# Loading the output weight ahead of the second chunk's v, in a fused attention and feed-forward kernel

## Chip, cores, metric

One core of one Trainium2 chip. The metric is the device time of one execution in microseconds (us). PE is TensorE (PEld its weight loads), DVE VectorE, ACT ScalarE, POOL GpSimd, SP SyncE. The executions whose state is on record are of the fast state, with a granted TensorE clock of 0.999 to 1.0.

## The reference

```python
def _attn_ref(q, k, v, tau):                       # q, k, v: (4, 6144, 256)
    qn = q / (np.linalg.norm(q, axis=1, keepdims=True) + 1e-06)
    kn = k / (np.linalg.norm(k, axis=1, keepdims=True) + 1e-06)
    s = kn.transpose(0, 2, 1) @ qn / tau           # 256 x 256 per batch
    ...                                            # softmax over the last axis
    return (v @ a).astype(np.float32)

def _moe_ref(x, w1, w2, w3, w_out):                # x: (24576, 256), d_ff 768
    h = np.maximum(np.maximum(x @ w1, x @ w2), x @ w3)
    return (h @ w_out).astype(np.float32)
```

## The kernel before

Per batch, a small gram product gives the attention matrix, which is folded into the three weights (`aw`). Then 48 chunks of 512 tokens stream by: load v (cast to bf16), transpose it, multiply by the three folded weights, take the maximum (`h_block`), multiply by the output weight `wo_sb` (`o_steps`). The output products of chunk n run between the hidden blocks of chunk n+1. All casting loads go out on GpSimd's queue; the transposes are DMA transposes issued by SyncE. The first chunk is transposed on PE.

The guard matters here: a one-element copy on GpSimd that reads the end of a transposed tile. The loads written after it go out only once it has run: in the trace of the kernel before, the transpose lands at 45.28 us, the copy starts at 45.35, and the next loads are issued at 45.57 and 46.39.

```python
    load_v(0)
    for fp in range(d_ff // FT):
        load_w(fp)                       # nine tiles of 128 KB
    load_v(1)
    wo_sb = consts.tile([P, FC, d_model], BF16, name="wo_sb")
    # ... gram of batch 0, softmax, v_transpose_pe(0), first third of aw ...
    v_transpose(1)
    guard = consts.tile([P, 1], BF16, name="guard")
    def hold_loads(gi):
        POOL.tensor_copy(out=guard, in_=vts[gi][:, TPC - 1, CC - 1, P - 1:P])
    hold_loads(1)
    POOL.dma_start(out=wo_sb, in_=moe_w_out.rearrange("(fc p) d -> p fc d", p=P))
    load_v(2)
    load_v(3)
    v_transpose(2)
    # ... main loop; chunk 0: 6 h_blocks, chunk 1: h_blocks with chunk 0's o_steps between
```

## Time and profile before

| | before |
|---|---|
| median (range) | 573.29 us (573.17 to 573.37), 3 runs |
| span of the profiled execution | 571.9 us, in a run of 573.68 us |
| PE busy | 552.9 us, 97% |
| hidden-layer products L378 | 1764 matmuls, 406.6 us |
| output products L398 | 1128 matmuls, 153.8 us |

Read it thus: PE is the bound from about 34 us on, so a wait counts only where PE has nothing to do. Note that the profiled execution was one of the slower ones, 0.4 us over the median; a span is to be compared with a span only with that in mind.

### The profile page before, as it was taken

How to read it: one execution, taken by the hardware profiler on the slowest of the kernel's cores; microseconds unless marked ns; L12 is line 12 of the kernel's file. 1: busy time of each engine (PE TensorE's matmuls, PEld its weight loads, DVE VectorE, ACT ScalarE, POOL GpSimd, SP SyncE). 2: the span in 40 equal slices, each digit the busy share in tenths (PEclk: the TensorE clock that was granted, in tenths of full speed). 3: DMA queues.
4: the chain of work that ended last, by engine and by line, in shares of the span. 5: the costliest groups of instructions: out<-in, count | busy, mean ns of one | idle time of the engine just before them, and what ended most of it. 6: DMA issues, size and time to landing. Idle time of an engine off the chain costs nothing.

```text
span 571.9 us, 9438 instructions
## 1 busy us (share of the span) xinstructions
PE 552.9 (97%) x3344; PEld 329.1 (58%) x3344; DVE 415.9 (73%) x658; ACT 309.1 (54%) x540; POOL 233.3 (41%) x237
## 2 busy tenths in 40 slices
PE   3799999999999999999999999999999999999997
PEld 2665555555755555555575555555575555555566
DVE  0048777777887777777767777777768778778775
ACT  1044567767464576776535467767635444444443
POOL 2442357776460078776560048777750000000000
PEclk9999999999999999999999999999999999999999
DMA  9997999895479268975279339985437333132112
GB/s 143 106 147 121 132 238 138 158 133 107 111 83 171 70 109 157 135 149 107 57 133 149 97 79 141 147 143 99 122 81 160 75 77 108 56 104 64 56 55 76
DMA packets 76960, 65.64 MB, mean 115 GB/s; under 512 B 52464, under 2 KB 62576, under 8 KB 76784
## 3 DMA queue, kind: packets, MB, share of 16 engines
q0 software_dynamic: 19072, 26.48, 39.1%
q1 hardware_dynamic: 57696, 38.41, 24.1%
q8 instruction: 26, 0.43, 0.3%
q14 instruction: 22, 0.18, 0.1%
q10 hardware_dynamic: 144, 0.13, 0.1%
HBM read 78.64 MB, written 25.17 MB: 182 GB/s over the span
## 4 chain that ended last, share of the span: by engine, by line
PE 90%; DMA 6%; issue 2%; POOL 1%; DVE 0%; POOLq 0%
PE h_ps L378 64%; PE o_ps L398 22%; DMA v_sb<-in_v_dram 3%; PE gram L249 3%; PE ew_ps L300 2%; DMA q_sb<-in_q_dram 1%; DMA wo_sb<-in_moe_w_out_dram 1%; DMA vt_sb<-v_sb 1%; POOL k_sb L99 0%; PE o_ps L423 0%; POOL w_sb L135 0%; POOL q_sb L102 0%; DVE o_sb L450 0%; POOL ident masks.py:199 0%; PE rs_ps L288 0%
## 5 line engine op out<-in xcount | busy, mean ns | idle before, releaser
L378 PE MATMUL h_ps<-vt_sb,aw_sb 128*128 128x512 bf16 (+1 forms) x1764 | 406.6, 375 | 0.1
L378 PEld LDWEIGHTS <-aw_sb 128*128 128x128 bf16 x1764 | 171.7, 98 | 161.7 <-DVE aw_sb L306 2.4
L383 DVE TENSOR_TENSOR s_mx<-h_ps,s_mx 128x512 bf16<-128x512 f32 (+1 forms) x294 | 198.8, 676 | 82.2 <-ACT s_mx L382 82.0
L382 ACT ACTIVATE s_mx<-h_ps 128x512 bf16<-128x512 f32 (+1 forms) x294 | 172.3, 586 | 124.3 <-PE h_ps L378 123.4
L384 DVE TENSOR_TENSOR ht_sb<-h_ps,s_mx 128x512 bf16<-128x512 f32 (+1 forms) x294 | 200.2, 681 | 30.6
L208 POOL TENSOR_TENSOR acc<-acc,sq 128x768 f32<-128x768 f32 x88 | 144.3, 1649 | 69.3 <-ACT sq L200 53.1
L398 PE MATMUL o_ps<-wo_sb,ht_sb 128*128 128x256 bf16 x1128 | 153.8, 273 | 0.1
L398 PEld LDWEIGHTS <-ht_sb 128*128 128x128 bf16 x1128 | 110.4, 98 | 52.2 <-issue 0.3
L401 ACT ACTIVATE o_sb<-o_ps 128x512 f32<-128x512 f32 x94 | 56.1, 597 | 83.9 <-PE o_ps L398 83.9
L110 POOL DMA_DIRECT2D v_sb<-in_v_dram x48 | 27.8, 584 | 37.4 <-DMA vt_sb<-v_sb 35.2
L200 ACT ACTIVATE sq<-q_sb 128x768 bf16<-128x768 fp8e4 x48 | 40.5, 844 | 0.0
L200 ACT ACTIVATE sq<-k_sb 128x768 bf16<-128x768 fp8e4 x48 | 40.1, 835 | 0.0
L205 POOL CAST acc<-sq 128x768 f32<-128x768 bf16 x6 | 4.9, 821 | 65.7 <-ACT sq L200 65.7
L102 POOL DMA_DIRECT2D q_sb<-in_q_dram x33 | 18.4, 565 | 4.1 <-DMA v_sb<-in_v_dram 3.1
L168 PE MATMUL kk<-k_sb 128*128 128x256 fp8e4 x48 | 7.5, 338 | 12.3 <-DVE k_sb L154 6.5
L99 POOL DMA_DIRECT2D k_sb<-in_k_dram x29 | 16.1, 557 | 2.9 <-issue 1.1
L249 PE MATMUL gram<-k_sb,q_sb 128*128 128x512 fp8e4 x144 | 16.8, 276 | 0.0
L249 PEld LDWEIGHTS <-q_sb 128*128 128x256 fp8e4 x144 | 15.9, 136 | 0.6
L303 ACT ACTIVATE aw_sb<-ew_ps,rinv 128x384 bf16<-128x384 f32 (+1 forms) x24 | 13.1, 554 | 5.7 <-PE ew_ps L300 4.8
L221 POOL PARTITION_ALL_REDUCE tot<-acc x6 | 10.9, 1858 | 11.9 <-DVE s_mx L383 6.0
L300 PE MATMUL ew_ps<-w_sb,et 128*128 128x384 bf16 (+1 forms) x96 | 15.6, 313 | 0.0
L168 PEld LDWEIGHTS <-k_sb 128*128 128x256 fp8e4 x48 | 6.4, 182 | 13.2 <-DMA k_sb<-in_k_dram 6.7
(64 smaller groups left out, 116.5 us busy)
## 6 DMA issues: line engine op xcount, KB each, us to landing
out_dram<-o_sb SPq DMA_DIRECT2D x41, 512.0 KB, 2.9
v_sb<-in_v_dram POOLq DMA_DIRECT2D x48, 256.0 KB, 4.4
k_sb<-in_k_dram POOLq DMA_DIRECT2D x24, 192.0 KB, 5.9
q_sb<-in_q_dram POOLq DMA_DIRECT2D x24, 192.0 KB, 7.3
out_dram<-o_sb SPq DMA_DIRECT2D x13, 256.0 KB, 2.0
k_sb<-in_k_dram POOLq DMA_DIRECT2D x5, 256.0 KB, 11.2
w_sb<-in_moe_w_dram POOLq DMA_DIRECT2D x9, 128.0 KB, 5.7
kf<-in_k_dram SPq DMA_DIRECT2D x1, 1024.0 KB, 5.0
```

The costliest lines, as they stand in the source:

```text
L102: POOL.dma_start(out=qk[b][0][:, g0:g0 + w, :], in_=q_r[b][:, g0:g0 + w, :])
L110: POOL.dma_start(out=t, in_=v_r[gi // NCH, gi % NCH])
L200: ACT.activation(out=sq, in_=src, func=AF.Square)
L208: POOL.tensor_tensor(out=acc, in0=acc, in1=sq, op=ALU.add)
L249: PE.matmul(g[:, j * C:(j + 1) * C], lhsT=qt[:, tsl, j * P:(j + 1) * P], rhs=kt[:, tsl, :], start=(tp == 0 and j == 0), stop=(tp == NG // ...
L300: PE.matmul(ew[:, :w], lhsT=et[:, j, ic * P:(ic + 1) * P], rhs=w_sb[m][:, j, fsl], start=(j == 0), stop=(j == CC - 1))
L378: PE.matmul(t.rearrange("p (t n) -> p t n", n=P), lhsT=aw[m][:, ic, fsl], rhs=vt[:, tsl, ic, :], start=(ic == 0), stop=(ic == CC - 1))
L382: ACT.activation(out=s_mx, in_=hp[0], func=AF.Copy)
L383: DVE.tensor_tensor(out=s_mx, in0=hp[1], in1=s_mx, op=ALU.max)
L384: DVE.tensor_tensor(out=ht, in0=hp[2], in1=s_mx, op=ALU.max)
L398: PE.matmul(st["ps"][:, half], lhsT=ht[:, fc, t * P:(t + 1) * P], rhs=wo_sb[:, fc, :], start=(fc == 0), stop=(fc == FC - 1))
L401: ACT.activation(out=st["o"][:, t - 1:t + 1, :].rearrange("p t d -> p (t d)"), in_=st["ps"], func=AF.Copy)
```

## The change

Its intent: let the output weight be there before PE asks for it, without waiting for the transpose of chunk 1. Nothing is added or removed.

```diff
     for fp in range(d_ff // FT):
         load_w(fp)
+    wo_sb = consts.tile([P, FC, d_model], BF16, name="wo_sb")
+    POOL.dma_start(out=wo_sb, in_=moe_w_out.rearrange("(fc p) d -> p fc d", p=P))
     load_v(1)
-    wo_sb = consts.tile([P, FC, d_model], BF16, name="wo_sb")
@@
     hold_loads(1)
-    POOL.dma_start(out=wo_sb, in_=moe_w_out.rearrange("(fc p) d -> p fc d", p=P))
     load_v(2)
```

## The prediction

> **What bounds the kernel now.** I read the page first: the busy line, the row of slices for PE, the chain that ended last by share.
>
> ```profile
> span 571.9 us, 9438 instructions
> ...
> PE 552.9 (97%) x3344; PEld 329.1 (58%) x3344; DVE 415.9 (73%) x658; ACT 309.1 (54%) x540; POOL 233.3 (41%) x237
> ...
> PE   3799999999999999999999999999999999999997
> ...
> PE 90%; DMA 6%; issue 2%; POOL 1%; DVE 0%; POOLq 0%
> ```
>
> TensorE is full in every slice after the first two, and it is 90% of the chain. What is not TensorE is the head, where data come in. The list of what PE waited for (its three groups) holds only the first gram's k and q tiles, 5.8 and 3.0 us from DMA and 6.5 us from a conversion. All of that is before 34.3 us and before the edited lines; the change touches none of it. So only the stretch from 36 to 59 us is in question, and there only PE's idle time counts. Next I read the chain in order of time for that stretch:
>
> ```profile
> 36.74 5.64 DMA v_sb<-in_v_dram
> 42.38 0.02 issue
> 42.39 2.89 DMA vt_sb<-v_sb
> 45.28 0.06 issue
> 45.35 0.18 POOL guard L469
> 45.53 0.04 issue
> 45.57 5.45 DMA wo_sb<-in_moe_w_out_dram
> 51.02 0.04 issue
> 51.07 0.27 PE o_ps L398
> ```
>
> Columns: start, length, what. The reader sees a serial path: v of chunk 1 lands at 42.38, its transpose at 45.28, a tiny GpSimd copy reads the transposed tile (the guard that holds back loads), and only then is the output weight issued. It lands at 51.02, and the first output product starts 0.05 us later. That is the whole chain which the change cuts. It looks like 14 us, but its length isn't what the kernel loses, because PE had other work alongside. The timeline of PE and of its weight loads over the same stretch gives the loss:
>
> ```profile
> 44.37 6.63 PE L378 MATMUL h_ps<-vt_sb,aw_sb 128*128 128x512 bf16 x30
> 51.07 0.82 PE L398 MATMUL o_ps<-wo_sb,ht_sb 128*128 128x256 bf16 x6
> 51.72 1.46 PE L378 MATMUL h_ps<-vt_sb,aw_sb 128*128 128x512 bf16 x6
> 53.01 0.82 PE L398 MATMUL o_ps<-wo_sb,ht_sb 128*128 128x256 bf16 x6
> ...
> 51.07 0.53 PEld L398 LDWEIGHTS <-ht_sb 128*128 128x128 bf16 x5 [0.35 <-issue]
> ```
>
> Six hidden-layer matmuls pace at 53.01 - 51.72 = 1.29 us, 0.215 each. Thirty from 44.37 end their slots at 44.37 + 30 x 0.215 = 50.82; the first output product could have started there and started at 51.07. So the wait for the weight costs **0.25 us** at most. The profile shows no PE wait for it, as each matmul's drawn length (0.38 us) covers the hole; the 0.35 us hole in the weight loads is its other trace.
>
> **What the Trainium skill says.**
> - Perfetto Trace Analysis, section Tensor Engine Instruction (MATMUL, LD_WEIGHTS): the profiler estimates a matmul's end from its size, it doesn't observe it. The trace agrees: matmuls 0.215 us apart are drawn 0.38 us long, so I take gaps from starts and not from ends.
> - DMA: Bandwidth & Descriptors, section Queues, rings and completion order: each DMA engine consumes one queue's descriptors in ring order. All the loads here go out on GpSimd's one queue, so a transfer put in front delays those behind by its own drain time. The trace agrees: in the backlog before chunk 1's v, six weight tiles land between 37.07 (29.87 issued + 7.2) and 41.14 (36.04 + 5.1), one every 0.68 us, and v 1.24 us after the last.
> - Same page, section Anatomy of one DMA: a fixed part of some 2.0 us per DMA plus bytes over a rate; the fixed part overlaps other transfers. The trace: the output weight alone takes 5.45 us from issue to landing, while a 128 KB tile inside the backlog adds 0.68. What counts for a tile queued in front is the second kind of number.
> - SBUF — State Buffer, section SBUF: two separate sides, the box on DVE blocking DMA: descriptors of a GpSimd-issued DMA are written by GpSimd and can starve while VectorE holds the shared port. The trace shows no such starvation here: issues of 0.70 to 0.83 us with VectorE busy beside them.
>
> **The change part by part.** No engine but GpSimd changes its order (I compared the two built programs): one DMA issue moves from behind the guard to ahead of chunk 1's v. Count and shapes stay.
>
> 1. *Removed wait.* The first output product no longer waits for 51.02. The weight is issued at 36.74 (where v is now), joins the backlog and lands about 41.14 + its drain. It is 384 KB in 1 KB source rows, as the weight tiles of 128 KB are, so 3 x 0.68 = 2.04 us: landing near 43.2, some 7.6 us before 50.82. Gain: 0.25 us, on the path.
>
> 2. *GpSimd issue.* The issue of the weight took 0.83 us, so v's issue goes from 36.74 to 37.57. It now waits for the semaphore of the third weight tile (issued 29.87, landed 37.07), which is earlier, so nothing is added. The queue is backlogged to 41 us; an issue at 37.57 still joins its tail with over 3 us to spare. Cost on the path: 0.
>
> 3. *Chunk 1's v behind the weight.* It lands at 42.38 + 2.04 = 44.42. SyncE's transpose then takes 2.89 us as now, since nothing else is in the queues beside it then or now: 47.31. Who needs it: the thirty matmuls at 44.37 are eighteen of chunk 0 (its last three blocks) and twelve of chunk 1, whose first starts at 44.37 + 18 x 0.215 = 48.24. **Slack now 48.24 - 45.28 = 2.96 us; after, 0.93 us.** Cost: 0, by a third of the present slack.
>
> 4. *Behind the guard.* The guard runs at 47.4 in place of 45.35, so v of chunks 2 and 3 is issued 2 us later, at 47.6 and 48.2, but without the weight in front. Now v of chunk 2 is issued at 46.39 and lands at 52.26; a v issued into an empty queue took 3.6 us (the one at 56.45), so it lands near 51.2, transposed by about 54.8 even at the slower 3.6 us of the transposes that share the queues. Chunk 2 starts on PE at 58.65 now (48.24 + 10.39 for a chunk, 0.25 of it the hole's). Later loads hang on the second guard (56.01 now), which comes some 1 us earlier. Cost: 0.
>
> Sum: -0.25 + 0 + 0 + 0. After 69 us PE is busy 499.2 of 502.9 us and waits for nothing in the list, so an early 0.25 us reaches the end undiluted. 573.29 - 0.25 = 573.0.
>
> **The rivals.**
> - *A new wait takes the place of the removed one:* chunk 1's transposed v comes too late. If v were delayed by the weight's whole 5.45 us, its tile would be ready at 50.73 and PE would idle 2.5 us: 573.29 - 0.25 + 2.5 = 575.5. For it: 0.93 us of slack is little, and the guard was put there by someone who wanted the transpose undisturbed. Against it: the tail of a backlogged queue pays drain time, not latency, and the bytes agree (192 GB/s written from 37.05 to 41.1; 393 KB / 192 = 2.05 us). If the drain is 1 us slower than that, the stall is 0.1 us.
> - *The backlog is worse than a sum:* more descriptors outstanding slow GpSimd's issue, or the slowest DMA engines fall behind. In the trace the last engines dribble for about 1 us after the bulk (40.9 to 42), also after the weight (bulk done near 50.0, landing 51.02), so the lag is there once and doesn't add up. If it did: stall near 0.1 to 1 us, 573.1 to 574.
> - *Hidden anyway:* the weight's wait is worth 0, as the page lists no PE wait for it. Then 573.3. The start times speak against it, but by a quarter of a microsecond only.
> - *An engine becomes the bound:* no compute engine gets an instruction more or less. Not credible.
>
> **Range and chances.** The mechanisms say -0.25, with an outside chance of +0.1 to +2.2. The runs of before spread 0.2 us (573.17 to 573.37), and another chip may differ by some tenths (my estimate). So 573.0, and 572.5 to 574.0 for eight in ten, the upper side wider because of the thin slack. Two per cent is 11.5 us: no rival comes near it. Faster 0.005, within 2% 0.985, slower 0.01.
>
> **What would show it.** Step 1: the weight lands near 43 us, the first output product directly follows thirty matmuls (start to start 6.45 us) and the hole in the weight loads is gone. Step 2: v issued near 37.6. Step 3: the transpose is issued near 44.4, lands near 47.3, and chunk 1's first matmul is not later than it was; a gap ahead of it with vt_sb as releaser would prove me wrong. Step 4: v of chunk 2 lands no later than 52.3. If the time is over 574, look for that gap first; if it is under 572.5, a wait in the head that I called untouched has moved.

## The result, and the profile after

| | before | after |
|---|---|---|
| runs, us | 573.29, 573.37, 573.17, 573.77 | 573.39, 573.27, 573.51, 573.50 |
| median, us | 573.33 | 573.44 |
| profiled span, us | 571.9 | 571.6 |

The ratio is 1.0 with a 95% interval of 0.9983 to 1.0018 (a ratio is the mean time of one kernel's fast runs over that of the other's fast runs of the same rounds, so not quite the ratio of the medians). The interval is plus or minus 1.0 us wide: a gain of 0.22 us could be in these times or not.

The two profiles are finer. First the chain that ended last of the kernel after, in order of time (start, length, what), in the stretch where before it ran through v, the transpose, the guard and the weight:

```profile
36.80 0.90 PE ew_ps L325 x8
37.69 1.41 PE h_ps L379 x6
39.11 1.31 PE ew_ps L301 x12
40.42 2.66 PE h_ps L379 x12
43.08 1.31 PE ew_ps L301 x12
44.39 6.54 PE h_ps L379 x30
50.93 0.66 PE o_ps L399 x6
```

No transfer is left in it from here on. The share line of the whole chain says the same: PE went from 90 to 93%, and the weight and v are gone from it.

```profile
PE 93%; DMA 5%; POOL 0%; issue 0%; DVE 0%; POOLq 0%
```

Next PE's timeline of the kernel after (start, length, engine, line, operation, count):

```profile
44.29 6.63 PE L379 MATMUL h_ps<-vt_sb,aw_sb 128*128 128x512 bf16 x30
50.77 0.82 PE L399 MATMUL o_ps<-wo_sb,ht_sb 128*128 128x256 bf16 x6
```

From the start of the thirty to the first output product it is 50.77 - 44.29 = 6.48 us; before it was 51.07 - 44.37 = 6.70. The hole of 0.22 us is gone. The single matmul starts agree: before, the last of the thirty and the first output product are 0.442 us apart, after 0.216, one ordinary step.

The spans differ by 0.30 us, and that adds up: the thirty start 0.08 us earlier, which is the head and not the change (the last matmul of the first gram already starts at 34.12 in place of 34.20, before the moved load is issued in either kernel), and 0.22 is the hole. The offset of 0.30 at the first output product is still 0.29 at the last block of output products, which is how one sees that nothing gave the gain back on the way. PE's last block, first of the kernel before and then of the one after:

```profile
566.18 2.13 PE L423 MATMUL o_ps<-wo_sb,ht_sb 128*128 128x256 bf16 x18
```

```profile
565.89 2.13 PE L424 MATMUL o_ps<-wo_sb,ht_sb 128*128 128x256 bf16 x18
```

Now the price. GpSimd's timeline of the kernel after:

```profile
36.66 0.88 POOL L141 DMA_DIRECT2D wo_sb<-in_moe_w_out_dram  x1
37.51 0.59 POOL L110 DMA_DIRECT2D v_sb<-in_v_dram  x1
48.12 0.19 POOL L470 COPY guard<-vt_sb 128x1 bf16<-128x1 bf16 x1 [10.02 <-DMA vt_sb<-v_sb]
48.36 1.08 POOL L110 DMA_DIRECT2D v_sb<-in_v_dram  x2
55.72 0.19 POOL L470 COPY guard<-vt_sb 128x1 bf16<-128x1 bf16 x1 [6.29 <-DMA vt_sb<-v_sb]
```

The guard runs at 48.12, where it was 45.35. And PE's weight loads of the kernel after:

```profile
47.53 0.31 PEld L379 LDWEIGHTS <-aw_sb 128*128 128x128 bf16 x2
48.11 2.32 PEld L379 LDWEIGHTS <-aw_sb 128*128 128x128 bf16 x12 [0.27 <-DMA vt_sb<-v_sb]
```

The bracket is the line to look at: the weight load of chunk 1's first product sat idle for 0.27 us until chunk 1's transposed tile was there. The matmul itself still started in its slot, at 48.175 after 47.959, one step of 0.216 us. The tile, landed at 44.38 + 3.69 = 48.07, came 0.1 us ahead of that matmul's start. So the margin to a stall is at most 0.1 us: the weight load, which in this row of matmuls starts 0.21 us ahead of its matmul, started only 0.065 us ahead of this one, and no run shows how much later it could have been. The change traded a wait of 0.22 us for a margin of at most 0.1 us.

### The profile page after: what moved, and what is told of

It is laid out like the page before. It is cut to its first block, busy times and chain, and to the rows that moved or that the text cites. A ratio compares the mean times of both kernels' runs of the same rounds, so it can differ in the third digit from the quotient of the medians.

```text
span 571.6 us, 9437 instructions
## 1 busy us (share of the span) xinstructions
PE 553.2 (97%) x3343; PEld 329.7 (58%) x3344; DVE 416.1 (73%) x658; ACT 309.5 (54%) x540; POOL 233.4 (41%) x237
## 4 chain that ended last, share of the span: by engine, by line
PE 93%; DMA 5%; POOL 0%; issue 0%; DVE 0%; POOLq 0%
PE h_ps L379 65%; PE o_ps L399 22%; DMA q_sb<-in_q_dram 5%; PE gram L250 3%; PE ew_ps L301 3%; POOL k_sb L99 0%; PE o_ps L424 0%; PE ew_ps L325 0%; PE warm_ps L459 0%; PE vt_ps L362 0%; PE gram L181 0%; DVE ht_sb L385 0%; DVE o_sb L451 0%; PE rs_ps L289 0%; PE gram L183 0%
## 5 line engine op out<-in xcount | busy, mean ns | idle before, releaser
L250 PE MATMUL gram<-k_sb,q_sb 128*128 128x512 fp8e4 x144 | 16.8, 276 | 0.0
L181 PE MATMUL gram<-k_sb,q_sb 128*128 128x512 fp8e4 x48 | 11.4, 331 | 2.8 <-DMA q_sb<-in_q_dram 2.7
```

The source lines that it names most:

```text
L250: PE.matmul(g[:, j * C:(j + 1) * C], lhsT=qt[:, tsl, j * P:(j + 1) * P], rhs=kt[:, tsl, :], start=(tp == 0 and j == 0), stop=(tp == NG // ...
```

## Experiments: what was designed, and what became of it

Four kernels were built on the two kernels as they are. They were not run: they set a matmul performance mode (the DoubleRow form in the gram products, which both original kernels use). The four designs were the change once more; the weight issued behind chunk 1's v but ahead of the guard; one more load of the weight's size ahead of that v; and the weight moved the other way. The last has no later version. Its edit against the kernel before:

```diff
-    POOL.dma_start(out=wo_sb, in_=moe_w_out.rearrange("(fc p) d -> p fc d", p=P))
     load_v(2)
     load_v(3)
+    POOL.dma_start(out=wo_sb, in_=moe_w_out.rearrange("(fc p) d -> p fc d", p=P))
```

> The weight moves the other way, from ahead of the v of chunks 2 and 3 to behind them. Theory A (the weight's landing is on the path of the kernel before, already at its first microsecond): it lands at 52.5 or later (two v at 1.27 us each in front, up to 2 us more if chunk 2's transpose is in the way), the first output product waits 1.65 to 3.7 us in place of 0.22, time 574.7 to 576.8. Rival (that wait is hidden, as the page lists none): within 0.3 us of 573.3.

Stand-ins without that mode followed. The gram products use ordinary matmuls over every second token group, so that the count of matmuls and their columns stay (the result is wrong). The edit that all of them share:

```diff
-            tsl = slice(2 * tp, 2 * tp + 2)
+            tsl = 2 * tp
@@
-                          ..., perf_mode=DR, skip_group_check=True)
+                          ..., skip_group_check=True)
```

They passed every check before the chip, but none was run: no chip took them, in eight submissions spread over about two hours, in groups of four and alone. Each is told with what it was to tell apart; nothing was measured in any.

The base, the kernel before with the shared edit alone:

> The kernel before with its gram products in the ordinary matmul mode, over every second token group only (a wrong result on purpose: half the tokens are left out, so that the count of matmuls and their columns stay). Base for the others of this group. Expected: the same head, thirty hidden-layer matmuls begin near 44.4 us, the weight lands near 51.0, the first output product starts 6.70 us after the thirty (0.22 late), transpose of chunk 1 in 2.9 us; time 573 to 574.5.

The change on that base (the diff of the change above):

> The change on top of that base. Theory A (the weight's wait was worth the 0.22 us hole and no more; chunk 1's v pays one drain time of 2.0 us): start of the thirty to first output product 6.48 us, v of chunk 1 near 44.4, span 0.2 to 0.3 us shorter than the base. Theory B (the gain is given back after 51 us): first product earlier, end of the span not. Theory C (the transpose took 3.7 us in place of 2.9 because an instruction fetch fell into its issue): 3.7 us again if a fetch falls within 44.4 to 46, else 2.9.

The weight behind chunk 1's v and ahead of the guard, which should keep the gain and pay nothing; it is the version that the profiles suggest as the best of the three orders, and it is untested:

```diff
-    load_v(1)
     wo_sb = consts.tile([P, FC, d_model], BF16, name="wo_sb")
+    load_v(1)
+    POOL.dma_start(out=wo_sb, in_=moe_w_out.rearrange("(fc p) d -> p fc d", p=P))
@@
     hold_loads(1)
-    POOL.dma_start(out=wo_sb, in_=moe_w_out.rearrange("(fc p) d -> p fc d", p=P))
```

> The weight is issued behind chunk 1's v, yet ahead of the guard: it costs v nothing. Theory A: v lands at 42.4 as in the base, the weight near 44.4, first output product 6.48 us after the start of the thirty, the slack of the transposed tile is back over 1 us; span as with the change within 0.2 us. Rival D (the reason for the guard: a load beside the transpose slows it much): transpose over 5.8 us, PE waits for it ahead of chunk 1, time over the base. Theory C: the issue of the transpose at 42.4 is free of the fetch near 45, so it is slowed by the weight's drain alone, at most 4.9 us to landing.

One more load of the same size ahead of that v, to double the delay and so measure the margin (its edit against x1_after):

```diff
     POOL.dma_start(out=wo_sb, in_=moe_w_out.rearrange("(fc p) d -> p fc d", p=P))
+    pad0_sb = consts.tile([P, FC, d_model], BF16, name="pad0_sb")
+    POOL.dma_start(out=pad0_sb, in_=moe_w_out.rearrange("(fc p) d -> p fc d", p=P))
     load_v(1)
```

> One more load of the weight's size (into a tile that nobody reads) ahead of chunk 1's v. Theory A: v 2.04 us later again, near 46.4. Theory C (the fetch near 45.2 is past): transpose in 2.9, landing 49.3 against a need at 48.2, PE idle 1.1 us, time 1.1 over the changed kernel's. If the slowness of 3.7 us comes with the lateness or with the queue and not with the fetch: landing 50.1, PE idle 1.9 us, time 1.9 over. Rival (slack is larger than the profile says, nothing waits): 0 over.

**A comparison that the traces contain.** One question of these can be followed without a new run: why chunk 1's transpose took 3.7 us from issue to landing after the change, and 2.9 before. Here are the two issues on SyncE's queue, before and then after (start, length):

```profile
42.39 1.34 SPq L354 DMA_TRANSPOSE vt_sb<-v_sb  x1
```

```profile
44.38 2.37 SPq L355 DMA_TRANSPOSE vt_sb<-v_sb  x1
```

And what the DMA engines moved in 40 slices from the issue to the landing, first before (42.4 to 45.4 us), then after (44.4 to 48.1 us):

```profile
GB/s 0 0 0 0 0 0 0 0 0 0 0 0 0 0 0 0 7 109 236 294 287 287 294 287 290 297 283 294 287 185 55 7 218 0 0 0 0 0 0 0
...
q8 instruction: 1, 0.02, 2.5%
```

```profile
GB/s 0 0 0 0 0 0 0 0 0 177 0 0 0 36 183 274 280 266 263 102 11 8 3 0 14 19 11 17 249 285 291 291 230 3 0 0 0 0 0 0
...
q8 instruction: 1, 0.02, 1.6%
```

Before, the data move in one block at about 290 GB/s, and the lone 16 KB instruction fetch on queue 8 (the 218 at the end) comes when they are through, at 44.86 us. After, the fetch (the 177) comes first, at 45.25 us, 0.9 us into the issue; then one half of the data, a break of about 0.8 us, and the other half. The data rate is the same, so this is no shortage of bandwidth, and no load on GpSimd's queue moved data in that time. The fetch took 0.96 us by the trace; the issue was 1.03 us longer than before.

Is that chance? Both traces hold 47 transposes, 94 in all. I counted, from the trace's own records, those with such a 16 KB fetch starting within their issue. Seven have it in the first 0.9 us:

| | issue, us |
|---|---|
| fetch starts 0.01 to 0.88 us into the issue (before: at 90.0, 110.8, 347.7; after: at 44.4, 110.5, 347.4) | 2.18 to 2.51 |
| the seventh such case, an exception (after, at 89.7; fetch 0.06 us in) | 1.53 |
| no 16 KB fetch in the issue, 84 transposes | 78 of them 1.26 to 1.57; six of 1.68 to 3.17, each with a load's packets on GpSimd's queue at the time |

(The remaining three: two of 13.8 and 14.4 us whose long issue holds a fetch in the middle, behind other traffic, and one of 1.47 with a fetch at its very end.) The same pair of lines can be read at one place of the kernel after: a transpose with a fetch at its start, and the next one without.

```profile
110.48 2.27 SPq L355 DMA_TRANSPOSE vt_sb<-v_sb  x1
120.43 0.33 SPq L408 DMA_DIRECT2D out_dram<-o_sb  x1
120.87 1.41 SPq L355 DMA_TRANSPOSE vt_sb<-v_sb  x1
```

So a transpose that meets a fetch is mostly some 0.9 us slower to issue (six of seven), in both kernels. Three of these six (at 90.0, 347.7 and 347.4) also had a load's packets on GpSimd's queue during the issue; the three clean ones are those at 44.4, 110.8 and 110.5.

The time from issue to landing is what PE depends on, and it gives a cleaner count. 59 of the 94 transposes have no load's packet between issue and landing. Of these, 41 have no instruction fetch in that time either (neither of 16 KB nor of the 8 KB that the other instruction queue moves), and all 41 land in 2.78 to 3.43 us. The other 18 have a fetch: ten land in 2.75 to 3.57 us, eight in 3.69 to 5.14. So every one of the 59 that took over 3.6 us had a fetch, but not every fetch made one late.

How the fetch could do it can be followed in the packet records for chunk 1's transpose. Its packets of 256 bytes take 0.018 us each. After, the fetch ends at 46.21. By 46.26, 21 packets of the transpose stand open; they stay so for 0.75 to 0.89 us, and all end between 46.98 and 47.03. Meanwhile packets go one at a time, about thirty of them, from the end of the fetch to 46.98. In the 0.2 us from 46.3 there are six, where the bulk of this transpose moves over 100 in 0.1 us:

```profile
DMA packets 6, 0.00 MB, mean 8 GB/s; under 512 B 6, under 2 KB 6, under 8 KB 6
```

Before, where the fetch comes at the end, no packet of this transpose takes over 0.018 us. This is what one late DMA engine would look like: a sixteenth of one half of the 1056 packets is 33, so the lone run has the length of one engine's share, done after the fetch, while the others wait for it. The Trainium skill says in DMA: Bandwidth & Descriptors, section Queues, rings and completion order, that each DMA engine changes between queues only after a whole packet; the 16 KB packet of 0.96 us would then hold up that engine's share, and these times agree. But the records carry no engine's number, so that it is one engine is inferred from the counts, and why the others wait isn't shown. It is also an observation and not an intervention: the kernel with one more load was meant to move the transpose past the fetch, and it did not run.

## Why the prediction was right or wrong

The range (572.5 to 574.0) holds the measured 573.44. That is a weak test: a forecast of no effect at all (573.29) would have passed it as well, so what counts is the steps. The number itself, 573.0, is 0.44 low, and the gain of 0.25 is not seen in the times: their medians stand 0.11 us the other way. Point by point:

- *Step 1, the removed wait.* In the profiled pair, right: 6.48 us for a stated 6.45, a gain of 0.22 for 0.25, and the weight landed at 36.66 + 6.4 = 43.06 for "near 43.2". The estimate of 2.04 us for its drain in the backlog held, where its 5.5 us alone would have misled.
- *Step 2, GpSimd's issue.* Right: v issued at 37.51 for 37.57, no wait before it.
- *Step 3, chunk 1's v.* Half right. v landed when SyncE could issue at 44.38, for 44.42. **The term that was mis-sized is the transpose: "2.89 us as now, since nothing else is in the queues beside it".** It took 3.69 us, so the tile was ready at 48.07 and not 47.31, and the slack was at most 0.1 us and not 0.93. "Nothing else" was said of loads and stores; an instruction fetch is a transfer too. Both executions have one near 45 us (at 44.86 before, 45.25 after), and moving the transpose by 2 us moved it onto that one. I could have seen it: a view of the kernel before (DMA from 44 to 45 us) that I had asked for ahead of the prediction lists it, inside the stretch into which the transpose was to move.

```profile
q8 instruction: 1, 0.02, 7.6%
```

The conclusion (no stall) held in this execution, but with about a tenth of the margin that I claimed, at most.
- *Step 4, behind the guard.* The direction was right and the times shifted by the same 0.8 us or so: v of chunk 2 issued at 48.36 for 47.6, landed by 51.97 for 51.2, in time against 52.26 before; the second guard at 55.72 for "some 1 us earlier" than 56.01, so 0.3. One sum there is wrong: a chunk takes PE 10.39 us without the hole (so it is after, 48.18 to 58.57) and took 10.61 with it, so chunk 2 started at 58.86 before and not at 58.65. The error was on the safe side.
- *"An early 0.25 us reaches the end undiluted."* Right in the profiled pair (0.30 at 51 us, 0.29 at 566). In the timed runs it can't be told. Two readings are left, and the data don't choose: the gain is there in each run and hidden by a spread of 0.2 to 0.6 us among equal kernels; or it is not there in each run. The second is possible because the wait was a near tie: before, PE was ready at about 50.84 and the weight at 51.02, so a shift of 0.2 us between the two would close the hole by itself, and after, a tile later by a little over 0.1 us would open another; this is argued, and no run shows it. I had taken one profile's hole for a constant.
- *The rivals.* Of a new wait taking the old one's place the first sign is there, the 0.27 us hole in the weight loads, without reaching the matmuls. That the backlog is worse than a sum is refuted in this trace: it was a sum to 0.1 us. "Hidden anyway" is wrong for the profiled pair and open for the timed runs.

## What to carry to other kernels

Before moving a load out of a long serial chain, measure what the bound engine loses at its end, by start times: here a chain of 14 us cost 0.22. Then reckon the load where it goes: in a backlogged queue it delays what is behind by its drain time (2.0 us here), not by its latency (5.5 us), and the margin of whatever it delays is the real price. A margin of 0.93 us read from one profile shrank here to at most 0.1 us, most likely through a transfer that nobody wrote in the program, an instruction fetch. So look in the stretch into which a transfer moves for every queue, the instruction queues too.

## What the Trainium skill lacked or had wrong

- Runtime: NRT & Kernel Launch, section Instruction fetch mechanics, says that instructions are refilled in 16 KiB blocks of 256, and calls the cost of crossing a block mostly hidden. The trace agrees on the size for one queue (26 fetches of 16,384 bytes; 26 x 256 = 6656, against PE's 3344 matmuls and 3344 weight loads); a second instruction queue moved 22 packets of 8,192 bytes. It lacks that a fetch can go with a slower DMA transpose beside it: 2.18 to 2.51 us to issue in six of seven cases with a fetch in the first 0.9 us, against 1.26 to 1.57 in 78 of 84 without one; and among transposes without a load beside them, 3.69 to 5.14 us to landing in eight of 18 with a fetch, against at most 3.43 in 41 without. The packet times point to the fetch as the cause; no experiment settled it.
- DMA: Bandwidth & Descriptors, section Anatomy of one DMA, gives a fixed 2.0 us plus bytes over 436e3 per us. For 384 KB written (twice that read, as f32 is cast to bf16) that makes an estimate of 2.9 or 3.8 us; issued into an empty queue, with two loads of v behind it, it took 5.5 us from issue to landing with 0.83 us of issue in it. The page doesn't say whether the bytes of a casting load are those read or those written. In the backlog here it was 192 GB/s written for bf16 and 104 for fp8, which is 384 and 416 GB/s of f32 read: the rates agree on the read side and not on the written side. These are two cases with other things different too, so that the read side sets the pace is a reading and not shown.
